# Decode block on one core: the output projection's partial products, the load of w3 and the column order of h are changed

## The chip, the cores and the metric

The kernel runs on one NeuronCore of a Trainium2 chip, in one launch. The metric is the device time of that core in microseconds (us). Before the change the median of three runs is 192.82 us (192.78 to 194.5). One more execution was recorded by the hardware profiler. It took 193.02 us, of which 191.6 us lie between the start of its first and the end of its last instruction (the span). All durations below come from that execution, and its times count from the start of the span.

## The reference

A block of one decode step for 8 sequences (B = 8, one token each, D = 512) in bf16: attention over the last 2048 rows of a key and value cache with 32 query heads and 8 key heads, then a small MLP.

```
h  = x + attention(layernorm(x) @ wq, k_cache[-2048:], v_cache[-2048:]) @ wo      # wo: 4096 x 512
x1 = layernorm(h) + hs                    # hs is zero: the token shift has nothing to shift with one token
h2 = h + x1 + gelu(layernorm(x1) @ w3) @ w4                # w3: 512 x 1792, w4: 1792 x 512
```

The caches are read from HBM: 8 sequences x 8 key heads x 2048 rows x 128 columns x 2 bytes for each of k and v, 67 MB in all. wq and wo have 4.2 MB each, w3 and w4 1.8 MB each.

## The kernel before, in words

**Loads.** SyncE (SP) issues all large loads on one DMA queue in a fixed order: wq, sixteen 2 MB tiles of k and sixteen of v interleaved, wo in three pieces (rows j 0 to 8, 8 to 24, 24 to 32 of each partition, `WO_AT`, 1, 2 and 1 MB), w3 (`load_w3`, L769), and w4 in three pieces (`load_w4`, L772: 8, 4 and 2 of its 14 blocks of 128 rows). Every piece has a semaphore, which the matmuls that read it wait for. A load of k or v waits for the buffer that it overwrites; wo, w3 and w4 wait for things that are long over. The queue works in order, and each load is spread over the 16 DMA engines, 8 partitions to an engine.

**Attention.** For each tile TensorE (PE) transposes k (L383), ScalarE (ACT) and VectorE (DVE) evict it, PE makes the scores (L408), the softmax runs on DVE and ACT, and PE multiplies by v (L504). The result for one sequence goes into `oW`, one column of 8 for each of 32 heads (j).

**After the last sequence** PE's instructions stand in this order; each engine runs its own list in order.

- `pe_x` (L562) puts x, turned, into `hT_ps`: four blocks of 128 columns of h, each as 128 partitions x 8 sequences.
- `pe_wo_row` (L549) multiplies heads j = 0 to 20 (`JR`) in rows: `oW` is the stationary operand (32 columns), 512 columns of wo are the moving one, and four heads run side by side in the four 32-column strips of the array. The sums lie in `hrow`, 4 x 32 partitions x 512.
- ACT copies `hrow` to bf16 (L559), and DVE subtracts that copy from it (L560), which gives the low half of the sum.
- `pe_wo` (L570) multiplies heads 20 to 32 in columns meanwhile: wo is the stationary operand in blocks of 128 x 128, and 8 columns of `oW` move. It adds into `hT_ps`.
- `pe_hr` (L579) adds both halves of `hrow`, turned, into `hT_ps`.
- `warm_end` (L490) issues products whose result nothing reads, 512 columns each, at places where PE would wait.
- The sum over columns (L649, L652), centring (L654, L656), squares (L658, L683). Then `pe_w3` (L673): 56 matmuls with a 128 x 128 block of w3 as the stationary operand. ACT and DVE make the gelu (L703, L705), POOL and DVE the rest of h (`fin`, L708 to L714).
- `pe_w4` (L728): for each of 14 blocks and four groups of 128 result columns a matmul with the gelu's 32 columns stationary and 128 columns of w4 moving; again four side by side. `pe_fin` (L718) adds h. DVE and ACT write the four groups of 128 columns to `out_sb` (L743, L745), and SP stores it.

h lies with column 128 k + p on partition p, block k. w3 is loaded in the same order, so a partition's data is four pieces of 1792 columns (3584 bytes), one from each of four rows of w3 that lie 128 rows apart. `w3_cols` (L666) takes the columns of w3 so that they fit w4's order: for 12 of the 14 blocks it reads every fourth column of w3 (a step of 8 bytes), for the last two every second.

Of the kernel before, what the change touches and what calls it, by code (L numbers as in the profile page):

```python
# [11 lines left out]
B = 8  # L12
# [10 lines left out]
FC = F // 128  # L23
FG = FC // 2
KC = D // 128
# [10 lines left out]
LQK = 2  # L36
JW = 32
WO_AT = (0, 8, 24, JW)
JR = 20
QS = NS // 2  # L40
QW = H - 2 * NQ * R + 1
QE = QW + NQ * R + NQ * R + QW
# [37 lines left out]
def bass_sequential_preLN__sliding_block_cached__mixer_s_mlp__decode_kernel(  # L80
# [19 lines left out]
    NITEM = NB * G  # L100
# [3 lines left out]
    with es:  # L104
# [13 lines left out]
        wo_v = wbig[:, :].rearrange("p (j n) -> p j n", j=JW)  # L118
        knat = sb([128, NK, CQ * DH], dt.bfloat16, "knat")
        vnat = sb([128, NV, CQ * DH], dt.bfloat16, "vnat")  # L120
        w3_sb = sb([128, KC, F], dt.bfloat16, "w3_sb")
        w4_sb = sb([128, FC, D], dt.bfloat16, "w4_sb")
# [13 lines left out]
        x_sb = sb([B, D], dt.bfloat16, "x_sb")  # L136
# [28 lines left out]
        oW = sb([128, JW, 32], dt.bfloat16, "oW")  # L165
        sel32 = sb([128, H], dt.bfloat16, "sel32")

        orow = sb([128, 2, 512], dt.bfloat16, "orow")
        hr = orow
# [16 lines left out]
        out_sb = orow[0:B, 0, :]  # L186
# [13 lines left out]
        sem_x, sem_wq, sem_w3, sem_out = (S(n) for n in ("sem_x", "sem_wq", "sem_w3", "sem_out"))  # L200
        sem_wo = [S(f"sem_wo{i}") for i in range(len(WO_AT) - 1)]
        sem_w4 = [S(f"sem_w4{i}") for i in range(3)]
        PE, AC, DV, PO, SP = (Engine(S(n)) for n in ("s_pe", "s_act", "s_dve", "s_pool", "s_sp"))

        def dma(eng, dst, src, sem, *waits):
            def f(e):
                e.dma_start(dst, src).then_inc(sem, 16)  # L207
            eng.op(f, *waits, inc=False)
# [20 lines left out]
        e = DV.op(lambda e: e.bn_stats(st6[:, :], x_sb[:, :]), X)  # L229
        e = DV.op(lambda e: e.bn_aggr(mv[:, :], st6[:, :]), e)  # L230
        e = PO.op(lambda e: e.tensor_scalar(rstd[:, :], mv[:, 1:2], EPS, None, ALU.add), e)
        e = PO.op(lambda e: e.tensor_tensor(rstd[:, :], rstd[:, :], half[0:B, 0:1], ALU.pow), e)
# [8 lines left out]
        e = DV.op(lambda e: e.tensor_reduce(hsq[:, :], ident_f[:, :].rearrange("p (u h) -> p h u", u=4), AX.X, ALU.add))  # L241
# [7 lines left out]
        e = DV.op(lambda e: e.tensor_reduce(rows16[:, :].rearrange("p (t r) -> p t r", t=KQ),  # L249
                                            rows_f[:, :].rearrange("p (t s r) -> p t r s", t=KQ, s=NS), AX.X, ALU.add))  # L250
# [12 lines left out]
        e = PE.op(pe_xT, e_xln, e_idb)  # L263
# [93 lines left out]
        e_Tlo, e_Thi, e_lo, e_hi, e_QK, e_PV = {}, {}, {}, {}, {}, {}  # L357
        e_negc, e_exp, e_P, e_PT, e_pT, e_wide = ({} for _ in range(6))
        e_acc, e_O, e_oX, e_oW = ({} for _ in range(4))
# [96 lines left out]
        LAST = NB - 1  # L456
# [33 lines left out]
        def warm_end(count):  # L490
            def f(e):
                for n in range(count):
                    ins = e.matmul(kbank[1], ident_b[:, :], still, start=True, stop=True)
                return ins
            PE.op(f, e_pT[LAST, 1])
# [49 lines left out]
        hT_ps = S_ps[0]  # L545
# [3 lines left out]
        def pe_wo_row(j0, j1):  # L549
            def f(e):  # L550
                for j in range(j0, j1):
                    u = j % 4
                    ins = e.matmul(hrow[32 * u:32 * (u + 1), :], oW[:, j, :], wo_v[:, j, :],  # L553
                                   start=(j < 4), stop=(j >= JR - 4),
                                   tile_position=(0, 32 * u), skip_group_check=True)
                return ins
            e = PE.op(f, e_oW[LAST], (sem_wo[min(j0 // WO_AT[1], 1)], 16), e_hi[NITEM - 1])
            if j1 == JR:
                e = AC.op(lambda e: e.activation(hr[:, 0, :], hrow, ACT.Copy), e)  # L559
                e_wo.append(DV.op(lambda e: e.tensor_tensor(hr[:, 1, :], hrow, hr[:, 0, :], ALU.subtract), e))  # L560

        def pe_x():  # L562
            def f(e):
                for nb in range(KC):
                    ins = e.matmul(hT_ps[:, nb * B:(nb + 1) * B], x_sb[:, nb * 128:(nb + 1) * 128],
                                   ident_b[0:B, 0:B], start=(nb == 0), stop=False, skip_group_check=True)
                return ins
            PE.op(f, free[0], X, e_idb)

        def pe_wo(j0, j1, piece):  # L570
            def f(e):
                for j in range(j0, j1):
                    for nb in range(KC):
                        ins = e.matmul(hT_ps[:, nb * B:(nb + 1) * B], wo_v[:, j, nb * 128:(nb + 1) * 128],
                                       oW[:, j, 0:B], start=False, stop=False, skip_group_check=True)
                return ins
            PE.op(f, (sem_wo[piece], 16))

        def pe_hr():  # L579
            def f(e):  # L580
                for part in range(2):
                    for nb in range(KC):
                        ins = e.matmul(hT_ps[:, nb * B:(nb + 1) * B], hr[:, part, nb * 128:(nb + 1) * 128], sel32[:, 0:B],
                                       start=False, stop=(part == 1), skip_group_check=True)
                return ins
            e_wo.append(PE.op(f, e_wo[-1], e_selb))
# [20 lines left out]
        e_qT, e_qturn = q_turn()  # L607
# [23 lines left out]
                        fill((p - LQK) // G + 2)  # L631
        pe_x()
        warm_end(2)
        pe_wo_row(0, WO_AT[1])
        pe_wo_row(WO_AT[1], JR)
        pe_wo(JR, WO_AT[2], 1)
        pe_wo(WO_AT[2], JW, 2)
        pe_hr()
        warm_end(1)


        v3 = lambda t: t.rearrange("p (n b) -> p n b", b=B)
# [2 lines left out]
        def bc(a):  # L645
            return bass.AP(tensor=a.tensor, offset=a.offset, ap=[a.ap[0], [0, KC], [1, B]])


        e = DV.op(lambda e: e.tensor_reduce(hsum[:, :], vr(hT_ps[:, 0:NH]), AX.X, ALU.add), e_wo[-1])  # L649
        e_hs = DV.op(lambda e: e.tensor_copy(hs[:, :], hT_ps[:, 0:NH]))  # L650
        msum, st2 = sm[:, 384:384 + B], o_rows[:, 0:NH]
        e_ms = PE.op(lambda e: e.matmul(msum, ones_f[:, :], hsum[:, :], start=True, stop=True), e)  # L652
        warm_end(2)
        e_u = DV.op(lambda e: e.scalar_tensor_tensor(v3(uT[:, :]), bc(msum), -1.0 / D, v3(hs[:, :]),  # L654
                                                     ALU.mult, ALU.add), e_ms, e_hs)
        e_hc = DV.op(lambda e: e.scalar_tensor_tensor(v3(hc[:, :]), bc(msum), -1.0 / D, v3(hs[:, :]),  # L656
# [16 lines left out]
        def pe_w3(lo, hi, *waits):  # L673
            def f(e):
                for fc in range(lo, hi):
                    n, f = divmod(fc, FH)
                    for kc in range(KC):
                        ins = e.matmul(y_ps[n][:, f * B:(f + 1) * B],
                                       w3_cols(kc, fc),
                                       uT[:, kc * B:(kc + 1) * B], start=(kc == 0), stop=(kc == KC - 1))  # L680
                return ins
            return PE.op(f, *waits)
        e_st2 = PE.op(lambda e: e.matmul(st2, ones_f[:, :], hsq[:, :], start=True, stop=True), e_sq,  # L683
                      free[2])
        warm_end(5)
        e_y = [pe_w3(0, FH, e_u, (sem_w3, 16)), pe_w3(FH, FC)]
        warm_end(4)

# [3 lines left out]
        e = AC.op(lambda e: e.activation(s2[:, :], vsum[:, :], ACT.Sqrt, bias=eps2[:, :], scale=1.0), e_vs)  # L692
# [8 lines left out]
        for n in range(2):  # L701
            cs = slice(n * FH * B, (n + 1) * FH * B)
            e = DV.op(lambda e, n=n, cs=cs: e.tensor_tensor(v3(g_x[:, cs]), v3(y_ps[n][:, 0:FH * B]), bcf(r2),  # L703
                                                            ALU.mult), e_y[n], e_r2)
# [3 lines left out]
        e = PO.op(lambda e: e.tensor_scalar(r1[:, :], vsum[:, :], EPS * (1.0 + EPS), None, ALU.add), e_vs)  # L708
        e = PO.op(lambda e: e.tensor_tensor(r1[:, :], r1[:, :], half[:, :], ALU.pow), e)
        e = DV.op(lambda e: e.tensor_tensor(v3(xb[:, :]), v3(hc[:, :]), bc(r1[:, :]), ALU.mult), e)  # L710
# [5 lines left out]
        z_ps = S_ps[1][:, 0:DH]  # L716
# [10 lines left out]
        for n, waits in enumerate(((*e_gT, free[1]), (), ())):  # L727
            lo, hi = W4_AT[n:n + 2]  # L728
            def pe_w4(e, lo=lo, hi=hi):
                for fc in range(lo, hi):  # L730
                    for nb in range(KC):
                        ins = e.matmul(z_ps[32 * nb:32 * (nb + 1), :], gT[:, fc, :],
                                       w4_sb[:, fc, nb * 128:(nb + 1) * 128], start=(fc == 0), stop=(fc == FC - 1),
                                       tile_position=(0, 32 * nb), skip_group_check=True)
                return ins
            if n == 1:
                pe_fin()
                warm_end(1)
            e_z = PE.op(pe_w4, (sem_w4[n], 16), *waits)
        for nb in range(KC):  # L740
            to, got = out_sb[:, nb * 128:(nb + 1) * 128], z_ps[32 * nb:32 * nb + B, :]
            if nb % 2:
                e_outa = AC.op(lambda e, to=to, got=got: e.activation(to, got, ACT.Copy), e_z)  # L743
            else:
                e_outd = DV.op(lambda e, to=to, got=got: e.tensor_copy(to, got), e_z)  # L745
# [21 lines left out]
                            ap=[[KC * H * DH, k], [KC * k * H * DH, 4], [1, QF]]), sem_wf, e_wz if n else None)  # L767

        def load_w3():  # L769
            dma(SP, w3_sb[:, :, :], B_w3.rearrange("(k p) f -> p k f", p=128), sem_w3, e_qturn)  # L770

        def load_w4(n):  # L772
            lo, hi = W4_AT[n:n + 2]
# [53 lines left out]
```

## Time and profile before

| | |
|---|---|
| median of 3 runs | 192.82 us |
| profiled execution | 193.02 us, span 191.6 us |
| busy: PE, DVE, ACT, POOL | 153.1, 116.5, 95.6, 13.7 us |
| DMA: bytes, mean rate | 79.38 MB, 414 GB/s |
| granted clock of PE, mean | 0.964 of full speed |
| last landing of a piece of w4 | 189.17 us |

PE, DVE, ACT and POOL are the computing engines, and PEld is PE's loading of the stationary operand, which overlaps its matmuls. L553 is line 553 of the kernel before. In the timeline a row is: start, duration of the whole group, engine, line, operation, what it writes and reads, sizes, how many, and in brackets how long the engine was idle before and what ended that. In the chain of waits a row is start, duration, and who held the end back in that stretch.

### The profile page before, as it was taken

To read this page: it belongs to the slowest core of one execution; us is meant where nothing else is said; L and a number is where in the kernel's file an instruction comes from. 1 tells how busy PE (TensorE), PEld (TensorE's weight loads), DVE (VectorE), ACT (ScalarE), POOL (GpSimd) and SP (SyncE) were. 2 spreads that over 40 slices of the span, in tenths; PEclk is the share of its full clock that TensorE was granted. 3 is DMA by queue.
4 is the path that set the end of the run, shared out by engine and by line. 5 is a ranking of instruction groups with operands and counts; after the bars stand their busy time and mean duration, and the time that the engine had idled before them with its cause. 6 is when DMAs were issued, how large, how long until landed. Compare 5 with 4: busy or idle time off the path is not lost.

```text
span 191.6 us, 3183 instructions
## 1 busy us (share of the span) xinstructions
PE 153.1 (80%) x1326; PEld 94.7 (49%) x1333; DVE 116.5 (61%) x259; ACT 95.6 (50%) x124; POOL 13.7 (7%) x37
## 2 busy tenths in 40 slices
PE   0049999598988988699978887889798895797895
PEld 0013866375556554465555455545554562343552
DVE  2733455834499368655885587558855886657423
ACT  3002667638357727284469255924782676340341
POOL 8400200100010001000100010002000000000040
PEclk9999999957999999789999999999999999699999
DMA  6999999999999999999999999999999999999991
GB/s 224 452 400 431 434 414 434 438 429 431 428 424 434 424 434 434 433 421 431 431 434 421 434 434 434 424 431 428 429 428 431 438 424 431 428 431 415 413 406 74
DMA packets 6477, 79.38 MB, mean 414 GB/s; under 512 B 688, under 2 KB 704, under 8 KB 1856
## 3 DMA queue, kind: packets, MB, share of 16 engines
q1 hardware_dynamic: 6448, 79.18, 97.3%
q8 instruction: 10, 0.16, 0.3%
q14 instruction: 3, 0.02, 0.0%
q10 hardware_dynamic: 16, 0.01, 0.0%
HBM read 79.18 MB, written 0.01 MB: 413 GB/s over the span
## 4 chain that ended last, share of the span: by engine, by line
DMA 55%; PE 20%; SPq 8%; DVE 8%; ACT 6%; issue 1%
DMA knat<-in_A_k_cache_dram 29%; DMA vnat<-in_A_v_cache_dram 11%; DMA w_sb<-in_B_w_dram 10%; SPq L207 8%; PE kT_ps L383 8%; DMA wbig<-in_A_wq_dram 6%; ACT kT_sb L393 3%; ACT pT_sb L472 3%; PE o_rows L504 3%; PE S_ps L504 3%; DVE kT_sb L395 2%; PE S_ps L302 2%; DVE oacc L516 2%; PE S_ps L408 2%; DVE omask L514 1%
## 5 line engine op out<-in xcount | busy, mean ns | idle before, releaser
L393 ACT ACTIVATE kT_sb<-kT_ps 128x1024 bf16<-128x1024 bf16 x64 | 65.6, 1025 | 54.9 <-PE kT_ps L383 54.7
L383 PE MATMUL kT_ps<-turn_f,knat 128*128 128x128 f32 x512 | 77.1, 291 | 13.8 <-DMA knat<-in_A_k_cache_dram 8.7
L383 PEld LDWEIGHTS kT_ps<-turn_f,knat 128*128 128x128 f32 x512 | 59.5, 147 | 35.0 <-issue 13.0
L395 DVE COPY kT_sb<-kT_ps 128x1024 bf16<-128x1024 bf16 x64 | 43.8, 685 | 25.4 <-PE kT_ps L383 25.2
L408 PE MATMUL S_ps<-kT_sb,qblk 128*32 128x512 bf16 x256 | 26.1, 401 | 2.7 <-ACT kT_sb L393 1.0
L504 PE MATMUL o_rows<-vnat,pT_sb 128*64 128x512 bf16 x128 | 16.5, 402 | 4.9 <-ACT pT_sb L472 4.9
L472 ACT ACTIVATE pT_sb<-o_rows,own_f 128x512 bf16<-128x512 f32 x28 | 17.7, 693 | 1.6 <-PE S_ps L408 1.2
L516 DVE TENSOR_REDUCE oacc<-omask 128x128 f32<-128x512 f32 x14 | 14.9, 1064 | 0.5
L504 PE MATMUL S_ps<-vnat,pT_sb 128*64 128x512 bf16 x112 | 13.4, 382 | 0.8 <-DMA vnat<-in_A_v_cache_dram 0.8
L504 PEld LDWEIGHTS o_rows<-vnat,pT_sb 128*64 128x64 bf16 x128 | 8.4, 114 | 11.3 <-issue 7.7
L350 POOL COPY qblk<-qT 64x64 bf16<-64x64 bf16 x16 | 5.0, 311 | 119.4 <-PE S_ps L408 106.4
L408 PEld LDWEIGHTS S_ps<-kT_sb,qblk 128*32 128x32 bf16 x256 | 6.6, 93 | 11.7 <-issue 6.9
L514 DVE TENSOR_TENSOR omask<-o_rows,own_s 128x512 f32<-128x512 f32 x7 | 4.8, 692 | 12.2 <-PE o_rows L504 12.2
L514 DVE TENSOR_TENSOR omask<-S_ps,own_s 128x512 f32<-128x512 f32 x7 | 4.8, 692 | 8.8 <-PE S_ps L504 8.8
L504 PEld LDWEIGHTS S_ps<-vnat,pT_sb 128*64 128x64 bf16 x112 | 5.8, 110 | 7.3 <-issue 2.0
L440 ACT ACTIVATE E_sb<-S_ps,negM 128x512 f32<-128x512 f32 x8 | 5.5, 689 | 6.5 <-DVE negM L436 6.5
L323 ACT ACTIVATE w_sb<-S_ps 128x512 bf16<-128x512 f32 x2 | 1.1, 594 | 11.4 <-PE S_ps L302 11.4
L259 PE MATMUL sm<-ident_b,xln_b 8*128 8x8 bf16 x4 | 0.3, 174 | 8.0 <-DVE xln_b L234 8.0
L529 PE MATMUL sm<-oacc,sel_o 128*128 128x256 f32 x16 | 6.1, 466 | 0.6 <-DVE oX L536 0.6
L431 DVE TENSOR_REDUCE mblk<-S_ps 128x1 f32<-128x512 f32 x8 | 5.5, 682 | 0.8 <-PE S_ps L408 0.8
L559 ACT ACTIVATE orow<-kT_ps 128x512 bf16<-128x512 f32 x1 | 0.6, 597 | 10.3 <-PE kT_ps L553 10.3
L453 DVE STREAM_TRANSPOSE PT_sb<-P_sb 128x512 bf16<-128x512 bf16 x8 | 5.6, 703 | 0.0
(118 smaller groups left out, 102.2 us busy)
## 6 DMA issues: line engine op xcount, KB each, us to landing
knat<-in_A_k_cache_dram SPq DMA_DIRECT2D x16, 2048.0 KB, 18.4
vnat<-in_A_v_cache_dram SPq DMA_DIRECT2D x15, 2048.0 KB, 20.1
wbig<-in_A_wq_dram SPq DMA_DIRECT2D x1, 3808.0 KB, 11.6
wbig<-in_A_wo_dram SPq DMA_DIRECT2D x2, 1024.0 KB, 22.5
knat<-in_A_v_cache_dram SPq DMA_DIRECT2D x1, 2048.0 KB, 19.8
wbig<-in_A_wo_dram SPq DMA_DIRECT2D x1, 2048.0 KB, 24.0
w_sb<-in_B_w_dram SPq DMA_DIRECT2D x1, 1792.0 KB, 29.9
w_sb<-in_B_w_dram SPq DMA_DIRECT2D x1, 1024.0 KB, 31.9
```

Source lines behind the costliest of these rows:

```text
L207: e.dma_start(dst, src).then_inc(sem, 16)
L383: ins = e.matmul(kT_ps[i % 2][:, n * 256:(n + 1) * 256].bitcast(dt.float32), knat[:, j % NK, c * DH:(c + 2) * DH].bitcast(dt.float32), tur ...
L393: e_lo[i] = AC.op(lambda e: e.activation(kT_sb[:, i % NKT, 0:W // 2], kT_ps[i % 2][:, 0:W // 2], ACT.Copy), e_Tlo[i], e_QK.get(i - NKT))
L395: e_hi[i] = DV.op(lambda e: e.tensor_copy(kT_sb[:, i % NKT, W // 2:W], kT_ps[i % 2][:, W // 2:W]), e_Thi[i], e_QK.get(i - NKT))
L408: ins = e.matmul(S_ps[b % 2][32 * t:32 * (t + 1), :], qblk[:, b % 2, KQ * q + t, half, at:at + H], kT[:, :, t, :, half], start=(q == 0 and ...
L431: e = DV.op(lambda e: e.tensor_reduce(mblk[:, 0:1], S_ps[b % 2][:, :], AX.X, ALU.max), e_QK[G * b + G - 1], e_mz)
L453: e_PT[b] = DV.op(lambda e: e.transpose(PT_sb[:, :], P_sb[:, :]), e_P[b], e_wide.get(b - 1))
L472: e_pT[b, t] = AC.op(lambda e: e.activation(pT_sb[:, b % 2, :, H * t:H * (t + 1)], bank[:, :].rearrange("p (n y) -> p n y", n=NN), ACT.Cop ...
L504: ins = e.matmul(bank[64 * u:64 * (u + 1), :], pT_sb[:, b % 2, n, :].rearrange("p (x q) -> p q x", q=NQ)[:, q, :], v_tile(m)[:, n * 512:(n ...
L514: free[at] = DV.op(lambda e: e.tensor_tensor(omask[:, :, :], bank.rearrange("p (s d) -> p s d", s=NS), own, ALU.mult), e_PV[m], e_acc.get( ...
L516: e_acc[m] = DV.op(lambda e: e.tensor_reduce(acc, omask[:, :, :].rearrange("p s d -> p d s"), AX.X, ALU.add), free[at], e_O.get(b - 2))
L529: e_O[b] = PE.op(lambda e: e.matmul(O_ps, sel_o[:, :], oacc[:, b % 2, :, :].rearrange("p q d -> p (q d)"), start=True, stop=True), e_acc[N ...
```

## The change

Five things differ.

1. **wo in rows.** All 32 heads go through `pe_wo_row`, in the three pieces of `WO_AT`, each waiting for its own load. `pe_wo` and `JR` are gone. The copy and the subtraction of `hrow` follow the last piece.
2. **Unused products.** The numbers in `warm_end` change: 5 new ones between the rows and `pe_hr`, 2 rather than 1 behind `pe_hr`, 3 rather than 2 behind the sum, 3 rather than 5 behind the squares.
3. **w3's load.** Partition p now takes rows 4p to 4p + 3 of w3, which lie together: one piece of 14336 bytes for a partition rather than four of 3584.
4. **h's order.** To fit that, column 4p + k of h lies on partition p, block k. `pe_x` and `pe_hr` read every fourth column as their stationary operand rather than 128 neighbours.
5. **w4 and the result.** `pe_w4` reads every fourth of the 512 columns of w4 as its moving operand, and the writes of `out_sb` go to every fourth column.

```
-                                   start=(j < 4), stop=(j >= JR - 4),
+                                   start=(j < 4), stop=(j >= JW - 4),
...
-            e = PE.op(f, e_oW[LAST], (sem_wo[min(j0 // WO_AT[1], 1)], 16), e_hi[NITEM - 1])
-            if j1 == JR:
+            e = PE.op(f, e_oW[LAST], (sem_wo[WO_AT.index(j0)], 16), e_hi[NITEM - 1])
+            if j1 == JW:
...
-                    ins = e.matmul(hT_ps[:, nb * B:(nb + 1) * B], x_sb[:, nb * 128:(nb + 1) * 128],
+                    ins = e.matmul(hT_ps[:, nb * B:(nb + 1) * B], x_sb[:, nb::KC],
...
-                        ins = e.matmul(hT_ps[:, nb * B:(nb + 1) * B], hr[:, part, nb * 128:(nb + 1) * 128], sel32[:, 0:B],
+                        ins = e.matmul(hT_ps[:, nb * B:(nb + 1) * B], hr[:, part, nb::KC], sel32[:, 0:B],
...
-        pe_wo_row(0, WO_AT[1])
-        pe_wo_row(WO_AT[1], JR)
-        pe_wo(JR, WO_AT[2], 1)
-        pe_wo(WO_AT[2], JW, 2)
+        for n in range(len(WO_AT) - 1):
+            pe_wo_row(*WO_AT[n:n + 2])
+        warm_end(5)
         pe_hr()
-        warm_end(1)
+        warm_end(2)
...
         e_ms = PE.op(lambda e: e.matmul(msum, ones_f[:, :], hsum[:, :], start=True, stop=True), e)
-        warm_end(2)
+        warm_end(3)
...
-        warm_end(5)
+        warm_end(3)
         e_y = [pe_w3(0, FH, e_u, (sem_w3, 16)), pe_w3(FH, FC)]
...
-                                       w4_sb[:, fc, nb * 128:(nb + 1) * 128], start=(fc == 0), stop=(fc == FC - 1),
+                                       w4_sb[:, fc, nb::KC], start=(fc == 0), stop=(fc == FC - 1),
...
-            to, got = out_sb[:, nb * 128:(nb + 1) * 128], z_ps[32 * nb:32 * nb + B, :]
+            to, got = out_sb[:, nb::KC], z_ps[32 * nb:32 * nb + B, :]
...
-            dma(SP, w3_sb[:, :, :], B_w3.rearrange("(k p) f -> p k f", p=128), sem_w3, e_qturn)
+            dma(SP, w3_sb[:, :, :].rearrange("p k f -> p (k f)"), B_w3.rearrange("(p k) f -> p (k f)", k=KC), sem_w3, e_qturn)
```

More of the change, by code (lines that the diff above doesn't have):

```diff
@@ L38 @@
 WO_AT = (0, 8, 24, JW)
-JR = 20
 QS = NS // 2
@@ L568, in pe_x @@
             PE.op(f, free[0], X, e_idb)
[L570 to L577, printed above, removed]
         def pe_hr():
```

## The prediction

> **What bounds the kernel now.** I read first the row of DMA busy shares on the page, then the chain of waits, then the timeline of the last 13 us. The busy row stands at nine tenths or more in every slice but the first and the last, so the loads never pause. The chain ends so:
>
> ```profile
> 162.99 6.97 SPq L207
> 169.96 0.04 issue
> 170.00 19.17 DMA w_sb<-in_B_w_dram
> 189.17 0.04 issue
> 189.22 0.32 PE S_ps L732 x8
> ```
>
> The end hangs on the last 256 KB of w4, which land at 189.17. Behind them stand eight matmuls, the write of the result and the store. So a step of PE counts only where it becomes later than a landing. The timeline shows how far each is from that:
>
> ```profile
> 178.96 1.26 PE L553 MATMUL kT_ps<-wbig,oW 128*32 128x512 bf16 x20 [0.39 <-DVE oW L542]
> 180.15 1.27 PEld L574 LDWEIGHTS S_ps<-oW,wbig 128*128 128x128 bf16 x48 [0.42 <-issue]
> 180.28 0.60 ACT L559 ACTIVATE orow<-kT_ps 128x512 bf16<-128x512 f32 x1 [10.29 <-PE kT_ps L553]
> 180.91 0.69 DVE L560 TENSOR_TENSOR orow<-kT_ps,orow 128x512 bf16<-128x512 f32 x1 [2.00 <-ACT orow L559]
> ...
> 183.53 1.24 PE L493 MATMUL kT_ps<-ident_f,ident_b 128*128 128x512 bf16 x5
> ...
> 184.93 1.87 PEld L678 LDWEIGHTS kT_ps<-uT,w_sb 128*128 128x128 bf16 x56 [0.65 <-DMA w_sb<-in_B_w_dram]
> ...
> 187.71 0.63 PE L732 MATMUL S_ps<-w_sb,qrow 128*32 128x128 bf16 x32
> ...
> 188.71 0.81 PE L732 MATMUL S_ps<-w_sb,qrow 128*32 128x128 bf16 x24
> 189.22 0.12 PEld L732 LDWEIGHTS S_ps<-w_sb,qrow 128*32 128x32 bf16 x8 [0.28 <-DMA w_sb<-in_B_w_dram]
> ```
>
> Three things are to be seen. The w3 matmuls (L678) started when w3 had landed (184.89 by the semaphore's last increment). The last unused product ahead of them started at 184.40; between such a product and the next kind of matmul the trace has 0.31 us (187.40 to 187.71), so PE was free at 184.71 and had 0.23 us to spare. Of the three pieces of w4 (32, 16, 8 matmuls) the first started behind unused products and so did the second (188.39 + 0.32); only the third waited, 0.28 us. That is all the room PE has before it sets the end itself.
>
> **w3's load.** Two stretches of the queue's row, the first with w3 alone (180.05 to 181.5), the second with packets of 8 and 16 KB (162.6 to 174):
>
> ```profile
> q1 hardware_dynamic: 160, 0.57, 96.6%
> ...
> q1 hardware_dynamic: 412, 4.96, 102.0%
> ```
>
> 0.57 MB in 96.6% of 16 engines x 1.45 us are 25.4 GB/s an engine; 4.96 MB in 102% of 16 x 11.4 us are 26.7. An engine's 114.7 KB of w3 take 4.51 us at the first rate and 4.30 at the second: 0.21 us. By the starts of an engine's packets (137 ns apart for 3584 bytes, 608 for 16 KB, so 532 for 14336) it is 32 x 137 - 8 x 532 = 0.12 us. All later landings come 0.1 to 0.2 us sooner, the last at about 189.0; I take 0.12. Were the long pieces cut up again, it would be nothing. SP issues the four loads between 155 and 174 us, long before they run, so fewer pieces to issue bring nothing.
>
> **wo in rows.** The trace has groups of four rows 216 ns apart. Eight groups from 178.96: the seventh needs wo's third piece, landed at 180.37, so it starts at 180.41, the eighth at 180.63, and it ends at 181.01, where the fifth ended at 180.22: +0.79 us for the copy behind it (0.60) and the subtraction (0.69). The 48 column products that go (1.35 us) lay beside these two and free nothing on the path. `pe_hr` then loads eight strided blocks: +8 ns each by the w3 rows below, 0.06. A second unused product behind it may hold the sum's matmul by 0 to 0.1; I take 0.05. So the squares come 0.90 us later, at 184.19. Behind them stand three unused products rather than five: 2 x 0.216 less. With the 0.23 to spare, w3's matmuls start 0.90 - 0.43 - 0.23 = **0.24 us later**, at 185.18, bound by PE and no longer by w3's landing. ACT's table load for the gelu (1.28 us behind the square root) moves 0.9, to about 186.47, and ends as the first half of w3's result is ready; POOL's power ends at 186.9, and DVE reads it behind the second half as now. Both stay hidden. The five new products cover 1.1 of the 1.4 us in which PE waits for the copy and the subtraction; the granted clock is 1.00 in every stretch from 178.9 us on, and the rows keep PE busier there, so I count no change of clock. `pe_x` lies ahead of the rows in an idle stretch of 0.4 us: nothing.
>
> **w4 at a step of four columns.** This is the term that decides. Today a group of four of these matmuls starts every 56 ns and reads 4 x 128 neighbours per partition. No moving operand in this trace has a step of 8 bytes, so it is bounded.
>
> - From below: the scores (L408) move 512 columns at a step of two, four side by side. Where two such groups follow each other, the second starts 215 ns after the first, as the rows of wo do. A step of 4 bytes is free, and 8 bytes may be: 56 ns.
> - From above: loads of stationary blocks. Of the 56 loads of w3 48 have a step of four columns, and they last 118 ns and come 33 ns apart. The eight with a step of two last 96 to 97 and come 25 apart, as wo's neighbours do (95 to 99). So a step of 8 bytes costs loads time that 4 bytes does not: 128 elements keep the reader 33 ns. Four matmuls side by side want 512 elements, 4 x 33 = 133 ns.
> - Between: the scores' group sweeps 4 x 512 x 4 bytes in 215 ns, 38 bytes a ns. At that sweep w4's group (4 x 128 x 8 bytes) takes 107.
>
> The loads are the nearest row: the only read of bf16 by PE at that step. Since a lone read of 128 fits into 56 ns and four may share only partly, I take 120, between the two shared figures. Then the 8 groups of the first piece take 0.51 us more, the 4 of the second 0.25, the last two 0.13 with the longer last one. The sum: 0.24 + 0.51 + 0.25 + 0.13, less the 0.28 of waiting that this fills, **+0.85 us**. The landings, 0.12 sooner, are then no longer what ends anything.
>
> [...]
>
> **The result's writes.** DVE's cast from 128 neighbours took 0.28 us; the cast at L245 writes 128 x 128 at a step of 8 bytes in 0.30, of 128 elements too. +0.02 each for two, below nothing not at all: +0.03.
>
> **Sum:** +0.88 us. The profiled execution (193.02) lies 0.2 above the median; I add to the median: 192.82 + 0.88 = **193.7**.
>
> **Rivals.**
>
> - *Step of four is free* (chance 0.36). PE reaches w4's third piece at 188.71 + 0.24 + 0.24 = 189.19, the landing at 189.05 + 0.04. It starts 0.03 sooner than now, the writes take 0.03 back: 192.8. For it: the scores' row. Against it: the loads' row. [...]
> - *Four streams in turn, each element a fetch of its own width* (0.07): a group takes 4 x 56 = 223 ns, and the sum is 0.24 + 1.34 + 0.67 + 0.33 - 0.28 + 0.03 = 2.3, 195.1. It passes the 1% from 202 ns a group on. Against it: a lone strided load needs 33 ns, not 53.
> - *A fetch of PE's code meets the last engine* (0.06). Packets of 16 KB on queue 8 occur at 180.76 and 187.31, and the first holds an engine for 0.95 us and slows its next two packets by 0.47. The second fell on an engine that had finished. 36 matmuls and their loads less, and five products more, put it some 62 instructions further on, near 188 us. Landing on the engine that is last would add up to 1.4: 194.2 with w4 unslowed, hardly more than 194.3 with it slowed. Most engines are done by then.
> - *The long pieces are no pieces* (in the others): w3 at today's rate costs the first rival 0.04 or less, since PE is there at 189.19, and the forecast nothing.
>
> **How the numbers follow.** Forecast 0.48 (193.1 to 194.1, from 70 to 133 ns a group and 0.1 to 0.35 for the delay), free step 0.36 (192.5 to 193.0: up to 0.3 of gain if PE's delay is hidden and 0.2 comes from the load), the other two 0.13, unknown 0.03. The range 192.5 to 194.2 leaves out the slow rival and half of the fetch. One per cent, 1.93 us, is about what a measurement of this kernel tells from no change; faster by that needs a landing that no row gives (0.02), slower the fetch rate of the second rival or two mishaps at once (0.12), within it the rest (0.86).
>
> **What would show it.** Groups of w4 more than 100 ns apart and no wait for w4's last piece, against 56 and a wait. L678 starting behind an unused product near 185.2. The last landing near 189.0. Packets of 14336 bytes at some 530 ns. `hrow`'s copy at 181.06. The prediction is wrong if w4's groups keep 56 ns, if the clock falls below 1.00 behind 179 us, or if w3 lands later than now.

## The result and the profile after

The changed kernel takes 193.87 us in the median of 22 runs (193.61 to 195.0), the kernel before 192.98 in as many (192.78 to 194.59). That is 0.89 us more by the medians. The ratio, from executions undisturbed on both sides, is 1.0035 with a 95% interval of 1.0019 to 1.0050: slower, by 0.2 to 0.5 per cent. The medians give 0.46; six executions of the kernel before took 193.5 us or more, which the ratio counts and the median hardly feels. The profiled execution took 194.14 us with a span of 192.8 (before: 193.02 and 191.6), so it lies 0.27 above the kernel's median, and its spans differ by more (1.2) than the medians do.

Line numbers move by 1 down to `pe_wo_row` and by 10 or 11 behind it: L552 is the rows' matmul (L553 before), L667 w3's (L678), L721 w4's (L732), L492 the unused products (L493), L732 and L734 the result's writes by ACT and DVE (L743 and L745).

The end of the chain of waits of the changed kernel (start, duration, who held the end back):

```profile
184.78 0.65 PE kT_ps L492 x3
185.43 1.77 PE kT_ps L667 x56
187.20 0.88 PE kT_ps L492 x4
188.08 1.05 PE S_ps L721 x29
...
189.57 0.86 PE S_ps L721 x16
190.43 0.02 issue
190.46 0.45 ACT orow L732
190.90 0.02 issue
190.92 0.45 ACT orow L732
```

Before, one row of 19 us of DMA led up to 189.17, and eight matmuls followed. Now no landing stands between 180.6 us, where wo's third piece lands, and the end. PE works through w3, unused products and w4 without waiting for a load, and two writes of 0.45 us close the chain. The timeline of the same kernel shows the pieces:

```profile
180.62 0.62 PE L552 MATMUL kT_ps<-wbig,oW 128*32 128x512 bf16 x8 [0.37 <-DMA wbig<-in_A_wo_dram]
181.29 0.60 ACT L558 ACTIVATE orow<-kT_ps 128x512 bf16<-128x512 f32 x1 [11.51 <-PE kT_ps L552]
...
184.61 0.81 PE L492 MATMUL kT_ps<-ident_f,ident_b 128*128 128x512 bf16 x3
...
185.26 1.94 PE L667 MATMUL kT_ps<-uT,w_sb 128*128 128x8 bf16 x56
...
188.01 1.12 PE L721 MATMUL S_ps<-w_sb,qrow 128*32 128x128 bf16 x32
...
189.50 0.89 PE L721 MATMUL S_ps<-w_sb,qrow 128*32 128x128 bf16 x24
190.46 0.92 ACT L732 ACTIVATE orow<-S_ps 8x128 bf16<-8x128 f32 x2 [2.72 <-PE S_ps L721]
190.46 0.90 DVE L734 CAST orow<-S_ps 8x128 bf16<-8x128 f32 x2 [2.24 <-PE S_ps L721]
```

The writes before the change:

```profile
189.56 0.56 ACT L743 ACTIVATE orow<-S_ps 8x128 bf16<-8x128 f32 x2 [2.13 <-PE S_ps L732]
189.56 0.60 DVE L745 CAST orow<-S_ps 8x128 bf16<-8x128 f32 x2 [1.65 <-PE S_ps L732]
```

The first 32 matmuls of w4 take 1.12 us where they took 0.63, the two last pieces run on without the wait of 0.28, and each engine's two writes take 0.9 where they took 0.6. By the starts in the record, w4's groups of four come 115 to 123 ns apart, but for the first gaps of the first two pieces, 94 and 99 (before: 55 or 56, but for a first gap of 65 or 66 in each piece). The last group starts at 190.07, where it started at 189.28: +0.79. With 0.09 of its own and 0.30 of writes that is the 1.2 of the spans.

w3's load came in the long pieces, as written. Between 180.2 and 181.35 us the queue moved nothing else:

```profile
q1 hardware_dynamic: 32, 0.46, 93.0%
```

32 packets in 93% of 16 engines x 1.15 us are 535 ns each, 26.8 GB/s an engine. The last piece of w4 landed at 189.11 (189.17 before), unnoticed.

### The profile page after: what moved, and what is told of

Its sections match the earlier page's. It is cut to its first block, busy times and chain, and to the rows that moved or that the text cites. A ratio compares the mean times of both kernels' runs of the same rounds, so it can differ in the third digit from the quotient of the medians.

```text
span 192.8 us, 3128 instructions
## 1 busy us (share of the span) xinstructions
PE 157.2 (82%) x1302; PEld 96.0 (50%) x1302; DVE 116.7 (61%) x259; ACT 96.0 (50%) x124; POOL 13.7 (7%) x37
## 4 chain that ended last, share of the span: by engine, by line
DMA 58%; PE 25%; DVE 8%; ACT 7%; issue 1%; SPq 0%
DMA knat<-in_A_k_cache_dram 29%; DMA wbig<-in_A_wo_dram 14%; DMA vnat<-in_A_v_cache_dram 10%; PE kT_ps L382 8%; DMA wbig<-in_A_wq_dram 6%; ACT pT_sb L471 4%; PE o_rows L503 3%; PE S_ps L503 3%; ACT kT_sb L392 2%; DVE kT_sb L394 2%; PE S_ps L301 2%; DVE oacc L515 2%; PE kT_ps L492 2%; PE S_ps L407 1%; PE sm L528 1%; DVE omask L513 1%
## 5 line engine op out<-in xcount | busy, mean ns | idle before, releaser
L382 PEld LDWEIGHTS kT_ps<-turn_f,knat 128*128 128x128 f32 x512 | 60.3, 148 | 33.3 <-issue 13.1
L528 PE MATMUL sm<-oacc,sel_o 128*128 128x256 f32 x16 | 7.1, 533 | 0.6 <-DVE oX L535 0.6
L492 PE MATMUL kT_ps<-ident_f,ident_b 128*128 128x512 bf16 x24 | 6.5, 380 | 0.0
```

What stands on the lines that cost most here:

```text
L382: ins = e.matmul(kT_ps[i % 2][:, n * 256:(n + 1) * 256].bitcast(dt.float32), knat[:, j % NK, c * DH:(c + 2) * DH].bitcast(dt.float32), tur ...
L528: e_O[b] = PE.op(lambda e: e.matmul(O_ps, sel_o[:, :], oacc[:, b % 2, :, :].rearrange("p q d -> p (q d)"), start=True, stop=True), e_acc[N ...
```

## The experiments

Where the time of a kernel is compared below, "before" is the kernel before, run on the same chip in turn with it. The changed kernel was not run again beside them: a difference to it is one between medians of separate series, in which the kernel before lay at 192.96 to 193.01 (192.98 beside the changed kernel).

### 1. w4 read as neighbours

```
-                                       w4_sb[:, fc, nb::KC], start=(fc == 0), stop=(fc == FC - 1),
+                                       w4_sb[:, fc, nb * 128:(nb + 1) * 128], start=(fc == 0), stop=(fc == FC - 1),
```

> The changed kernel, but w4's moving operand is read as 128 neighbours, as before the change (the result's columns then don't belong together; the work is the same). If the step of four columns is what slows w4, its groups of four start 56 ns apart again instead of 118, the last piece of w4 is bound by its landing or nearly so, and the last group starts about 0.8 us sooner (189.3 instead of 190.09): the kernel is 0.8 us faster than the changed one and 0.3 to 0.4 us slower than the one before, by the result's writes and PE's delay. If the groups are slow for another reason (a lower clock, late code, PE's later start), they stay near 118 ns and the time does not move.

193.17 us in the median of 12: 0.70 less than the changed kernel, where about 0.8 was expected. The ratio does not tell it from the one before (1.0003, 0.9988 to 1.0019); the medians are 0.21 apart, where 0.3 to 0.4 was expected. Its timeline:

```profile
188.54 0.79 PE L721 MATMUL S_ps<-w_sb,qrow 128*32 128x128 bf16 x24
189.04 0.12 PEld L721 LDWEIGHTS S_ps<-w_sb,qrow 128*32 128x32 bf16 x8 [0.27 <-DMA w_sb<-in_B_w_dram]
189.39 0.92 ACT L732 ACTIVATE orow<-S_ps 8x128 bf16<-8x128 f32 x2 [2.12 <-PE S_ps L721]
```

The groups stand 56 ns apart again, and the wait for w4's last piece is back. The writes are still the slow ones, but that piece landed at 189.00 in this execution, so they begin 0.17 sooner than before (189.56). The step is what slows w4.

### 2. and 3. The result to neighbours, and both

```
-            to, got = out_sb[:, nb::KC], z_ps[32 * nb:32 * nb + B, :]
+            to, got = out_sb[:, nb * 128:(nb + 1) * 128], z_ps[32 * nb:32 * nb + B, :]
```

> The changed kernel, but the four groups of the result are written to neighbouring columns (the order of the columns is then another). The forecast had 0.03 us for these writes; the profile of the changed kernel shows DVE and ACT at 0.45 us for each of two writes rather than 0.28 and 0.27. If the step of 8 bytes is what slows them, they take 0.28 again and the kernel is 0.3 us faster than the changed one. If they are slow because of what runs beside them, 0.45 stays and the time does not move.

193.63 us (12 runs), 0.24 less than the changed kernel (0.3 was expected); DVE's two writes take 0.59, ACT's 0.56. The third kernel has this edit and that of the first:

> The changed kernel with both of its last reads and writes in neighbours, so that only wo's rows, the unused products, w3's load and the strided x and hr are left of the change (the result's columns are not the reference's). If the step of w4 and that of the writes are all that costs time, the kernel is within 0.1 us of the one before: PE's delay of 0.3 at w3 fits into the 0.28 of waiting for w4's last piece, and that piece lands 0.1 sooner. If wo's rows cost more than was worked out, it is 0.2 to 0.4 us slower than the one before.

192.95 us (12 runs) against 192.96, ratio 0.9986 (0.9967 to 1.0005): no difference. The single edits, 0.70 and 0.24, add up to 0.94, against the 0.92 of both together. Its chain of waits names PE alone:

```profile
186.88 0.88 PE kT_ps L492 x4
187.77 0.56 PE S_ps L721 x32
...
188.76 0.59 PE S_ps L721 x24
189.35 0.02 issue
189.37 0.28 DVE orow L734
```

But the loads of the last eight matmuls do not follow those before them:

```profile
189.02 0.12 PEld L721 LDWEIGHTS S_ps<-w_sb,qrow 128*32 128x32 bf16 x8
```

The last piece of w4 landed at 188.98, and they start 0.04 behind it, as they do before the change (189.17 and 189.22). By the record they stood idle 0.10 us until then, less than the chain names as a wait. So the landing bounds this kernel, and 0.10 us of PE's room is left. In the changed kernel the same loads did not wait at all.

### 4. The rows of wo alone

The kernel before with `pe_wo` replaced by rows, and with the changed numbers of unused products (parts 1 and 2).

> The kernel before with parts 1 and 2 of the change alone: all of wo in rows, and the unused products. w3, h, w4 and the result stay as before, so the result is the reference's. If PE's delay is hidden by the wait for w4's last piece, it is 0 to 0.1 us slower than the kernel before, with w3's matmuls at 185.1 to 185.3 instead of 184.94. If the delay reaches the end, 0.2 to 0.4.

192.94 us (12 runs), ratio 0.9992 (0.9978 to 1.0007): no difference. w3's matmuls start 0.17 later than before, and the timeline shows no wait for w4's last piece any more:

```profile
185.11 1.94 PE L667 MATMUL kT_ps<-uT,w_sb 128*128 128x8 bf16 x56
...
188.85 0.58 PE L721 MATMUL S_ps<-w_sb,qrow 128*32 128x128 bf16 x24
189.48 0.56 ACT L732 ACTIVATE orow<-S_ps 8x128 bf16<-8x128 f32 x2 [1.90 <-PE S_ps L721]
```

The delay fits into the former wait of 0.28. By the record 0.05 us of it is left: the last eight matmuls start at 189.14, 0.04 behind the landing at 189.09. That landing is 0.08 sooner than in the profile of before, and so are the writes (189.56 there), though w3 is loaded here as before.

### 5. w3's load alone

The kernel before with the line of `load_w3` from the change.

> The kernel before with part 3 alone: w3 comes in one run of 14336 bytes per partition, and nothing else is changed (h then does not fit w3, so the result is not the reference's). Worked out from packets, the last engine is 0.12 us sooner, and this kernel is bound by the last landing: 0.1 to 0.2 us faster than the one before. If the gain is lost among the engines, whose last landings differ by some 0.1 us between executions anyway, no difference shows.

192.75 us in the median of 12 against 193.01, but the ratio is 0.999 with an interval of 0.9961 to 1.0018: a gain is not shown by the times. The chain of waits of its profile:

```profile
188.97 0.04 issue
189.01 0.33 PE S_ps L732 x8
```

There the landing is at 188.97, 0.20 sooner than in the profile of before, of which 0.12 were worked out from packets. Among the twelve profiles with the long pieces it lies between 188.90 and 189.19, in the middle at 188.99; the two with the short ones have 189.17 and 189.09 (fourth experiment). The size fits, but single executions differ by as much. Better than "0 to 0.3 us" the runs don't say.

### 6. Steps of two and of eight

w4's moving operand takes every second column, or every eighth across two blocks:

```
-                                       w4_sb[:, fc, nb::KC], ...
+                                       w4_sb[:, fc, 256 * (nb // 2) + nb % 2:256 * (nb // 2 + 1):2], ...      # step two
+                                       w4_flat[:, 512 * min(fc, hi - 2) + nb:512 * min(fc, hi - 2) + 1024:8], ...  # step eight
```

> The changed kernel, but w4's moving operand takes every second column of one half of the 512 instead of every fourth (the result is then not the reference's; as many columns move). If the four streams side by side share one reader that is just filled at a step of 4 bytes, as the scores suggested, a group of four takes 56 ns, as neighbours do. If any step at all costs time in these short matmuls, it lies between 56 and 118 ns.

> The changed kernel, but w4's moving operand takes every eighth column, 16 bytes apart, across two blocks of w4 (the result is then not the reference's). If the cost goes by the bytes that the four streams sweep, a group takes twice the 118 ns of a step of 8 bytes, about 235. [...] If a step above 4 bytes has one fixed price, it stays near 118.

By their starts, and behind the first gap of each piece, the groups stand 56 to 59 ns apart at step two and 226 to 240 at step eight. All matmuls of w4 (duration in ns: shortest, median, longest), first step two, then step eight:

```profile
L721 PE MATMUL S_ps<-w_sb,qrow x56: 217/219/234, 187.5 to 189.0; 128*32 128x128 bf16 x56
```

```profile
L722 PE MATMUL S_ps<-w_sb,qrow x56: 385/407/433, 187.8 to 191.3; 128*32 128x128 bf16 x56
```

Of the steps tried, 4 bytes is all but free (56 to 59 ns, against 56 with neighbours in the first experiment), and above that the time grows with the step: 117 at 8 bytes, about 230 at 16. One execution each; the kernels took 192.98 and 195.45 us (before beside them: 193.06).

### 7. One strip at a time

The two loops of `pe_w4` change places, once with w4 at a step of four and once with neighbours:

```
-                for fc in range(lo, hi):
-                    for nb in range(KC):
+                for nb in range(KC):
+                    for fc in range(lo, hi):
```

> The changed kernel with w4's matmuls in another order: all blocks of a piece for one group of result columns, then the next group, so that neighbours in the list use the same strip of the array and cannot run side by side. The result is the same. If four streams share a reader and a lone one at a step of 8 bytes has room (33 ns for 128 elements by the strided loads, against 53 of array time), a matmul takes no longer than the same order with neighbours, which runs beside this one. If each stream is slow by itself, it takes about 118 ns, twice as long as with neighbours.

> The yardstick for the lone streams: the same order, one strip at a time, with w4 read as neighbours (the result's columns then don't belong together). About 56 ns for a matmul of 128 columns if the array's own time is the limit, more if the change of the stationary operand in one strip is.

The 53 ns of array time are an estimate: unused products of 512 columns follow each other 215 or 216 ns apart in the profile of before, and a quarter of that is 54.

The first 0.46 us of w4 in each (busy time and number of matmuls and loads, granted clock, DMA), first the step of four, then neighbours:

```profile
187.78:188.24 0.46, 0.46 (x6) 0.46 (x7) 1.00 0.24 94
```

```profile
187.90:188.36 0.46, 0.46 (x12) 0.46 (x13) 1.00 0.24 94
```

Half as many matmuls. Behind a first gap of 94 ns with the step and 65 with neighbours, the next three are 117, 116 and 116 ns with the step and 56, 55 and 57 with neighbours. (Further on two matmuls start 5 to 17 ns apart; the first ones are alone.) One execution each; the kernels took 195.3 and 194.0 us. So **a lone stream is slow by itself** (116 to 117 ns), and four side by side, at 117, are no slower than one. The theory of the shared reader falls. By these starts a stream sweeps 128 x 8 bytes in 117 ns and, four side by side, 128 x 16 in about 230, 8.8 to 8.9 bytes a ns; 128 x 4 bytes take 56 to 59 ns, 8.7 to 9.1 bytes a ns, hardly more than the 56 of neighbours. That each stream is held to about 9 bytes a ns is the author's estimate from these four runs (the changed kernel, the steps of two and eight, the lone stream); it fits them, but no run shows a limit itself, nor what would set it.

### 8. Why the writes are slow

ACT writes its two groups at the same step into another part of the tile:

```
-            to, got = out_sb[:, nb::KC], z_ps[32 * nb:32 * nb + B, :]
+            to, got = orow[0:B, nb % 2, nb::KC], z_ps[32 * nb:32 * nb + B, :]
```

> The changed kernel, but ACT writes its two groups of the result at the same step of four columns into another part of the tile, so that DVE and ACT no longer write between each other's elements (half of the result is then missing). If DVE and ACT hinder each other because they write into the same 8 bytes at the same time, the writes fall from 0.45 to about 0.28 to 0.30 us each. If a lone write at a step of 8 bytes from PSUM is slow, 0.45 stays.

The timeline has 0.92 us for ACT's two and 0.90 for DVE's two, as in the changed kernel. They don't hinder each other by writing between each other's elements. (One execution, 193.98 us.) The last kernel lets no two writes run at the same time:

> The changed kernel up to w4, and in place of the result's four writes ten writes of 8 x 128 elements, one at a time: DVE from PSUM to neighbours and at a step of 2, 4 and 8 elements, DVE from SBUF to neighbours and at a step of 4, then ACT from PSUM to neighbours and at a step of 2, 4 and 8 (the result is then not the reference's, and the end is later by the added writes). If a write at a step of 8 bytes is slow by itself, DVE takes 0.45 us at step 4 against 0.28 for neighbours with ACT idle. If it is slow only because DVE and ACT write the same partitions at the same time, it takes 0.28 to 0.30 alone. If it is PSUM as the source that matters, the write from SBUF stays at neighbours' time, as the cast at 128 x 128 before the change (0.30 us at this step) suggested.

Its timeline, in the order of that list:

```profile
190.04 0.28 DVE L731 CAST orow<-S_ps 8x128 bf16<-8x128 f32 x1 [2.20 <-PE S_ps L721]
190.35 0.29 DVE L732 CAST orow<-S_ps 8x128 bf16<-8x128 f32 x1
190.68 0.43 DVE L733 CAST orow<-S_ps 8x128 bf16<-8x128 f32 x1
191.14 0.71 DVE L734 CAST orow<-S_ps 8x128 bf16<-8x128 f32 x1
191.88 0.21 DVE L735 CAST orow<-E_sb 8x128 bf16<-8x128 f32 x1
192.13 0.30 DVE L736 CAST orow<-E_sb 8x128 bf16<-8x128 f32 x1
192.46 0.27 ACT L737 ACTIVATE orow<-S_ps 8x128 bf16<-8x128 f32 x1 [5.11 <-DVE orow L736]
192.76 0.30 ACT L738 ACTIVATE orow<-S_ps 8x128 bf16<-8x128 f32 x1
193.10 0.44 ACT L739 ACTIVATE orow<-S_ps 8x128 bf16<-8x128 f32 x1
193.57 0.73 ACT L740 ACTIVATE orow<-S_ps 8x128 bf16<-8x128 f32 x1
```

A write at a step of 8 bytes is slow alone, on both engines alike: 0.28, 0.29, 0.43 and 0.71 us at 2, 4, 8 and 16 bytes on DVE, 0.27, 0.30, 0.44 and 0.73 on ACT. From SBUF the step of 8 bytes costs 0.09 (0.21 to 0.30) where from PSUM it costs 0.15. If PSUM alone mattered, the write from SBUF would not change; it does. Why the source makes a difference was not tried. (One execution, 197.11 us with the ten writes.)

### 9. A version without the steps

> A version that keeps w3's long pieces and the rows of wo without a step in w4 or the result: h is made in both orders, the strided one for w3 and the one of 128 neighbours for the squares, the rest of h, w4 and the result. That costs 4 + 8 short matmuls and one copy on DVE in places where both wait; three unused products are taken out, so that PE reaches w3, and w4's last piece, before they land. If w3's load is worth 0.1 to 0.2 us at the end, it is that much faster than the kernel before: about 192.8. If not, it equals it.

```
+                    ins = e.matmul(hN_ps[:, nb * B:(nb + 1) * B], x_sb[:, nb * 128:(nb + 1) * 128],
+                                   ident_b[0:B, 0:B], start=(nb == 0), stop=False, skip_group_check=True)
...
+                        ins = e.matmul(hN_ps[:, nb * B:(nb + 1) * B], hr[:, part, nb * 128:(nb + 1) * 128],
+                                       sel32[:, 0:B], start=False, stop=(part == 1), skip_group_check=True)
...
+        e_hn = DV.op(lambda e: e.tensor_copy(hn[:, :], hN_ps), e_wo[-1])
```

Besides, the centred copy for the squares and `fin` take `hn`, w4 and the result are read and written as before the change, and three unused products go (one each behind `pe_hr`, the squares and w3).

192.88 us in the median of 12 against 193.01, ratio 0.9985 (0.9969 to 1.0001). It is faster than the changed kernel (by 1.0 us in the medians), and against the one before a gain of 0.1 is likely but not shown. In its profile PE still reached w3 only at 185.31 (landed at 184.83), later than was meant. But the last landing is what bound the end:

```profile
189.24 0.12 PEld L739 LDWEIGHTS S_ps<-w_sb,qrow 128*32 128x32 bf16 x8
```

These loads start 0.04 behind the landing of w4's last piece at 189.19, the latest of all profiles here, after 0.09 us of idling by the record. Taking out more unused products would therefore have gained nothing in this execution.

## Why the prediction was right

Forecast were 193.7 us, measured are 193.87; forecast was +0.88 against the median shown, measured +0.89 between the medians. By its steps:

- **The end passes from the DMA to PE: right.** The wait for w4's last piece is gone, and the chain of waits shows no landing in the last 12 us. The granted clock stayed at 1.00 behind 178.9 us, as was assumed.
- **w3 in long pieces: right in size, and as little worth as was said.** 535 ns a packet against 532 worked out (and 32 x 137 - 8 x 532 is 0.13 rather than 0.12). The last landing came 0.07 sooner in this profile, covered by PE, and 0.20 in the fifth experiment's; that the long pieces did this is not shown.
- **wo in rows and the unused products: +0.24 us at w3, measured +0.32** (184.94 to 185.26), +0.17 in the fourth experiment. Two things differ. wo's third piece landed at 180.58 in this execution, 0.21 later than in that of before, and the rows waited for it. And PE had more room than was worked out: the 0.31 us between an unused product and the next kind of matmul came from ahead of w4, but ahead of w3 it is 0.22 (185.05 to 185.26), so 0.32 us were to spare and not 0.23. What this term hangs on shows in ten profiles with the same list on PE up to w3: in eight w3 starts 4.68 to 4.69 us behind the landing of wo's third piece, and in two (the first experiment and the writes alone) a little later, 0.05 behind w3's own landing. From the landing of before, 180.37, that gives 185.06, +0.12. That these parts alone cost nothing, because the wait of 0.28 takes it in, the fourth experiment shows.
- **w4's step: right in size, wrong in its reason.** 120 ns a group forecast, 117 measured. Taking the step out gives 0.70 back; the sum had +0.85 up to the end of w4, the profile has +0.79 at the last group's start and +0.88 at its end. But the step argued that four streams share one reader, with a lone stream unharmed, and took 120 as a middle between 107 and 133. The lone stream is as slow as the four. The figure came out because 107 is the 215 ns put down for the scores times 128 x 8 over 512 x 4 bytes, and this quotient, a half, is the same for each stream by itself as for four together; measured, the lone stream took 117 ns against 56. Besides, the 215 ns of the scores is not what the trace has: two of their groups follow each other only once, 230 ns apart from start to start, where wo's first two rows' groups are 227 apart. That 4 bytes is all but free stands, as the sixth experiment shows.
- **The step at which four fetches for each element would push the kernel over 1%** (the slow rival) was put at 202 ns; its own sum gives about 195. 117 is far from either. The last packet of 16 KB on queue 8, which the forecast took for PE's code (the profile calls its kind "instruction"), came at 189.04 instead of near 188, when the queue's last packet for w4 (188.81) was over, and cost nothing that shows.
- **A free step of four** (the rival with 192.8): the runs decide against it for TensorE's moving operand. At a step of 8 bytes the groups are 117 ns apart, with neighbours 56 (first experiment); 56 to 59 is what a step of 4 bytes has (sixth).
- **The result's writes: mis-sized.** +0.03 forecast, +0.30 in the profile, 0.24 by the second experiment. The step took 0.30 us, a cast from SBUF at this step, and set it beside 0.28, a cast of neighbours from PSUM. Both differ from the other case in two things, and each hid the other: from SBUF neighbours would have taken 0.21, from PSUM the step takes 0.43 alone.

That the sum still fits is in part luck. The writes cost 0.2 to 0.27 more than forecast. Against that, the delay at w3 is mostly smaller than in the profile of the changed kernel: in the nine other profiles with the same list w3 starts between 184.74 and 185.15, in the middle at 185.02, which is 0.08 later than before, where +0.24 was forecast. That start is 0.24 sooner than in the profile of the changed kernel, and that profile lies 0.27 above its median. The two misses are of opposite sign and cancel in good part.

## What to carry to other kernels

When a load is rearranged into longer runs, ask which operand takes over the stride: here 0.12 us of DMA time, as worked out, was bought with 0.70 us on TensorE and 0.24 on the writes, by the medians of the first two experiments, at the very end, where nothing hides them. A duration from another place of the profile is a yardstick only together with its own counterpart without the edit, from the same source and to the same place. And a part that adds work may be free while it fits into one wait (here 0.17 us at w3 into 0.28, in the fourth experiment); count that wait once, and see which part fills it first. Whether a landing still bounds the end is best read from starts: in the third, fourth and ninth experiment a wait of 0.1 us or less does not appear in the views of waits, but the matmuls behind it start 0.04 us after the landing.

## What was not expected of the hardware

In these runs a stride of the moving operand cost a lone stream as much as four side by side. With 128 columns of bf16 a lone matmul took 55 to 57 ns with neighbours and 116 or 117 at a step of 8 bytes (seventh experiment), a group of four 56 (first experiment) and 115 to 123 (the changed kernel). Groups of four took 56 to 59 at 4 bytes and 226 to 240 at 16 (sixth). DVE and ACT slowed down alike when they wrote bf16 at a step, one write at a time (eighth): 0.28, 0.29, 0.43, 0.71 us for 8 x 128 elements from PSUM at 1, 2, 4 and 8 elements (DVE), 0.27, 0.30, 0.44, 0.73 (ACT).
